# Linear attention and a long convolution on one core: rows regrouped by nine, heads stacked in pairs, the inverse transform by two half sums

## The chip, the cores and the metric

The kernel runs on one core of one Trainium2 chip. The metric is the device time of one execution in microseconds (us); lower is better. A core has five engines that run on their own and wait for each other by semaphores: TensorE (PE in the profile, with its weight loads shown as PEld), VectorE (DVE), ScalarE (ACT), GpSimd (POOL) and SyncE (SP). Matmuls accumulate in PSUM, eight banks of 128 partitions by 512 fp32 numbers. Loads that change fp32 into bf16 are issued from POOL's queue, transposes by DMA and the stores from SP's queue.

## The reference

```python
def phi(x):                                  # q, k, v: batch 8, heads 8, seq 576, head_dim 64
    proj = x @ w_phi                         # 64 -> 128 features
    proj = proj - max(abs(proj), axis=-1)
    return concat([exp(proj), exp(-proj)])
q_p, k_p = phi(q), phi(k)
kv  = k_p.T @ v        # per head, 256 x 64
z   = sum(k_p, over s)
x   = (q_p @ kv) / (q_p @ z + 1e-6)          # heads side by side: batch 8, seq 576, 512
x1, x2, x3 = split(x @ w_proj)               # 512 -> 3 * 512
conv = irfft(rfft(x2) * rfft(filter))        # along the sequence, length 576
out  = (x1 * conv * x3) @ w_out              # 512 -> 512, float32
```

## The kernel before

The program is one list of words, `PLAN`, and `run` (line 874) carries out the words one after another; each word is a method of `Kernel` that issues a few instructions, and `@n` names the PSUM bank. The order of the words is thus the order of the instructions on each engine, and an engine takes its instructions strictly in that order. Work of two batches is interleaved: while batch b goes through the projections and the convolution, batch b+1 goes through the attention.

**Attention of a batch.** `load` and `loadt` (L492, L499) bring k, q and v on POOL's queue, `tr` and `trt` (L505, L512) transpose k and q on SP's queue. 576 rows do not divide into tiles of 128 rows, so row s = 4p+j of the first 512 rows sits on partition p, and the last 64 rows of the eight heads are "tail" tensors of their own (`knt`, `kTt`, `Etp`, `vtp`, `xnt`, ...). `Pk` and `Qn` (L522) project k and q through w_phi; `maxk` and `maxq` (L582, L595) take the absolute maxima on DVE; `ex` (L570) the exponentials on ACT. The maximum of q has to be taken away inside the exponential: `mhi` and `mlo` split it into two bf16 parts, `trm` (L622) transposes them by DMA into `mT`, and `Pq` (L549, L553) adds them by a small matmul. `mT` is therefore the gate into the second half of a batch's attention, and its eight transposes mark the eight batches in the profile. `em` and `vs` (L627, L635) scale v; `KV` (L663, L666) forms k_p.T @ [v, 1] with all 128 rows as contraction plus a tail matmul, `NE` (L684) multiplies with q_p, `rc` and `xn` (L698, L703) divide, `trx` (L722) transposes the result by DMA into `xT`.

**Projections and convolution.** The Fourier transform is cut by parity: `fold` (L739, POOL) forms sums and differences of the two halves of the sequence, `X2` (L755, PE) projects them, `F` (L434) multiplies with the cosine and sine matrices `fwd`, with `Fe` copying to `C`. `m1`, `m2` and `m3` (L771, L779, L785) multiply with the filter's spectrum, `A` and `B`: m1 on DVE, m2 on POOL, their sum m3 on DVE into `Y`. `I` (L837) is the inverse transform over all 512 first rows, with five matmuls of 512 columns for each quarter of the features, and `It` (L844) the same for the 64 tail rows. `X1`, `X3` (L791), `X1t`, `X3t` (L798) are the two gates: `X1e` copies the first, `tm` (L827) multiplies it with the second into `ts`, `ym` (L848) multiplies `I`'s result with `ts`, `O` (L858) multiplies with w_out in five pieces a batch, the fifth with 64 rows only, and `Oe` and `st` write out.

**Setup.** The transform matrices are made on the chip (`gen_*`), the filter is loaded by 26 DMAs on SP's queue ahead of the first transposes (L402, L407), folded on POOL and transformed (`H`).

Number of buffers (`RING`): two each of `kn`, `qn`, `vn`, `xn`, `xT`; one each of `kT`, `qT`, `eo`, `x2n`, `C`, `t1`, `t2`, `Y`, `x1s`, `ts`, `yT`.

Of the kernel before, what the change touches and what calls it, by code (L numbers as in the profile page):

```python
# [19 lines left out]
RING = {'Ekp': 4, 'Ekm': 4, 'Eqp': 3, 'Eqm': 3, 'vp': 3, 'vm': 3, 'r': 4, 'o': 4, 'kn': 2, 'qn': 2, 'vn': 2, 'knt': 2, 'qnt': 2, 'vnt': 2, 'mk': 2, 'mkt': 2, 'mq': 2, 'mh': 2, 'mT': 2, 'xT': 2, 'xTt': 2, 'KVs': 2, 'vtp': 2, 'vtm': 2, 'Etp': 2, 'Etm': 2, 'etp': 2, 'etm': 2, 'rt': 2, 'kTt': 2, 'qTt': 2, 'xnt': 2, 'xn': 2}  # L20
# [16 lines left out]
Pq,0,3@4 rc,0,0@2 xn,0,0@2 loadt,q,2 ex,q,m,0,3@4 tr,q,1 NE,0,2@6 trx,0,0 rc,0,2@6 Pk,1,1@0 xn,0,2@6
NEt,0@2 ex,q,p,0,3@4 trt,q,1 trx,0,2 Pk,1,0@6 maxk,1,1@0 loadt,k,2 NE,0,3@4 ex,k,m,1,0@6 rc,0,3@4
xn,0,3@4 ex,k,p,1,0@6 load,k,3 trx,0,3 Pk,1,2@4 rct,0@2 xnt,0,1@2 ex,k,p,1,2@4 load,q,3 xnt,0,0@2
trxt,0 Qn,1,0@2 maxk,1,0@6 loadt,q,3 ex,k,p,1,1@0 maxq,1,0@2 Qn,1,1@6 em,p,1,0 fold,0,1 em,m,1,0  # L40
ex,k,m,1,1@0 maxq,1,1@6 trt,k,1 X1,0,0@2 ex,k,m,1,2@4 Qnt,1@0 maxqt,1@0 Qn,1,2@6 foldt,0,1 X2,0,2@3
maxk,1,2@4 X1e,ACT,0,0@2 foldt,0,0 X2,0,3@0 vs,p,1,0 X2e,ACT,0,2@3 maxq,1,2@6 X2e,ACT,0,3@0 X2,0,4@1
X2e,ACT,0,4@1 Qn,1,3@4 maxq,1,3@4 Pk,1,3@2 X1,0,1@0 fold,0,0 ex,k,m,1,3@2 tr,k,2 F,0,2@6 mhi,1
maxk,1,3@2 Fe,ACT,0,2@6 F,0,3@7 X2,0,1@1 X1e,ACT,0,1@0 vs,m,1,0 Fe,DVE,0,3@7 X2,0,0@4 em,m,1,1
X2e,ACT,0,1@1 X2e,ACT,0,0@4 X3,0,1@5 mlo,1 vs,m,1,1 trm,1 F,0,1@6 tm,0,1@5 em,p,1,1 ex,k,p,1,3@2
Pkt,1@0 F,0,4@7 trt,q,2 maxkt,1@0 Fe,ACT,0,1@6 emt,p,1 vs,p,1,1 trt,k,2 F,0,0@4 emt,m,1 Fe,DVE,0,4@7
Fe,ACT,0,0@4 Pqt,1@0 Pq,1,1@2 ext,m,1@0 Pq,1,0@6 vst,p,1 X3,0,0@5 ext,p,1@0 X1,0,2@4 tm,0,0@5
vst,m,1 ex,q,m,1,1@2 X1e,DVE,0,2@4 Pq,1,2@0 X3,0,2@5 m1,0,1 ex,q,m,1,2@0 load,v,3 KV,1,1@4 m1,0,2
# [12 lines left out]
X2,1,0@2 maxk,2,2@4 vs,m,2,0 X2e,ACT,1,0@2 F,1,2@3 maxq,2,2@6 Fe,ACT,1,2@3 Pk,2,3@0 F,1,1@4 tr,k,3
# [855 lines left out]
```

## Time and profile before

| | |
|---|---|
| time, median of 3 runs | 421.32 us (417.97 to 423.01) |
| the profiled execution's own time | 419.22 us |
| its span in the profile | 417.2 us |
| granted TensorE clock, mean | 0.942 |
| matmuls | 3367 |
| DMA: packets, moved | 111598, 43.90 MB |
| of these smaller than 512 B | 80648 |

A line of a group names the line in the code, the engine, the operation, what it writes and reads, shapes and count; then the busy time of all of them in us and the mean duration of one in ns, then the engine's idle time just ahead of them and what ended it. A line of a stretch gives its length, then for PE, PEld, DVE, ACT and POOL the busy us and the number of instructions, the granted TensorE clock, the mean busy share of the 16 DMA engines (over 1 where transfers queue) and GB/s. A timeline line gives start and duration in us; for SP's queue the duration is that of the issue, not of the transfer. A line of the chain gives start, duration, and line of a piece of the chain that ended last.

### The profile page before, as it was taken

How to read it: one execution, taken by the hardware profiler on the slowest of the kernel's cores; microseconds unless marked ns; L12 is line 12 of the kernel's file. 1: busy time of each engine (PE TensorE's matmuls, PEld its weight loads, DVE VectorE, ACT ScalarE, POOL GpSimd, SP SyncE). 2: the span in 40 equal slices, each digit the busy share in tenths (PEclk: the TensorE clock that was granted, in tenths of full speed). 3: DMA queues.
4: the chain of work that ended last, by engine and by line, in shares of the span. 5: the costliest groups of instructions: out<-in, count | busy, mean ns of one | idle time of the engine just before them, and what ended most of it. 6: DMA issues, size and time to landing. Idle time of an engine off the chain costs nothing. (4 is left out here: it accounts for less than half of the span.)

```text
span 417.2 us, 8401 instructions
## 1 busy us (share of the span) xinstructions
PE 323.1 (77%) x3367; PEld 176.0 (42%) x3367; DVE 270.1 (65%) x426; ACT 222.5 (53%) x340; POOL 226.7 (54%) x237
## 2 busy tenths in 40 slices
PE   5001277079696988779979979588999999989995
PEld 5001137034462446434635545234654564446452
DVE  3605945355884776925857999537889788876172
ACT  1201677528535637646816777246656756765532
POOL 8580738089924893078725780378428805760540
PEclk9999997559898999969989999979999999999999
DMA  9999959984989377856896394814833234103403
GB/s 157 221 194 183 123 92 117 133 113 85 118 104 162 72 97 71 130 129 80 98 157 152 74 115 77 155 41 81 111 83 102 53 70 128 42 2 46 126 2 113
DMA packets 111598, 43.90 MB, mean 105 GB/s; under 512 B 80648, under 2 KB 105736, under 8 KB 111560
## 3 DMA queue, kind: packets, MB, share of 16 engines
q0 software_dynamic: 39232, 16.29, 33.9%
q1 hardware_dynamic: 72328, 27.08, 32.9%
q8 instruction: 26, 0.43, 0.4%
q14 instruction: 12, 0.10, 0.1%
HBM read 34.01 MB, written 9.44 MB: 104 GB/s over the span
## 5 line engine op out<-in xcount | busy, mean ns | idle before, releaser
L791 PE MATMUL ps<-xT,wproj 128*128 128x512 bf16 x256 | 66.5, 393 | 10.7 <-DMA xT<-xn 8.2
L595 DVE TENSOR_REDUCE mq<-ps 128x8 f32<-128x1024 f32 x32 | 38.5, 1219 | 31.8 <-PE ps L522 27.0
L582 DVE TENSOR_REDUCE mk<-ps 128x8 f32<-128x1024 f32 x32 | 38.6, 1216 | 26.0 <-PE ps L522 20.6
L739 POOL TENSOR_TENSOR eo<-xT 128x896 bf16<-128x896 bf16 x16 | 30.1, 1885 | 36.3 <-DMA xT<-xn 36.3
L755 PE MATMUL ps<-wproj,eo 128*128 128x512 bf16 (+1 forms) x160 | 41.9, 405 | 6.0 <-POOL eo L739 5.9
L779 POOL TENSOR_TENSOR t<-C,B 128x512 bf16<-128x512 bf16 x32 | 38.8, 1228 | 13.5 <-ACT C L671 11.3
L570 ACT ACTIVATE Ekm<-ps 128x1024 bf16<-128x1024 f32 x32 | 32.4, 1023 | 20.8 <-PE ps L522 20.2
L570 ACT ACTIVATE Ekp<-ps 128x1024 bf16<-128x1024 f32 x32 | 32.4, 1020 | 20.5 <-PE ps L522 15.6
L570 ACT ACTIVATE Eqm<-ps 128x1024 bf16<-128x1024 f32 x32 | 32.5, 1031 | 17.1 <-PE ps L553 17.1
L837 PE MATMUL ps<-inv,Y 128*128 128x512 bf16 x160 | 39.5, 388 | 1.6 <-DVE Y L785 1.6
L635 POOL TENSOR_TENSOR vp<-vn,vp 128x1024 bf16<-128x1024 bf16 x16 | 30.8, 1930 | 15.9 <-ACT vp L627 15.8
L858 PE MATMUL ps<-wout,yT 128*128 128x512 bf16 x160 | 38.9, 386 | 0.0
L791 PEld LDWEIGHTS <-wproj 128*128 128x128 bf16 x256 | 23.1, 99 | 29.3 <-issue 6.8
L492 POOL DMA_DIRECT2D qn<-in_q_dram x8 | 7.3, 912 | 51.1 <-DMA qT<-qn 41.9
L671 ACT COPY o<-ps 128x512 f32<-128x512 f32 (+1 forms) x31 | 18.1, 585 | 31.1 <-PE ps L858 24.3
L522 PE MATMUL ps<-wphi,qT 64*128 64x128 bf16 x256 | 14.5, 245 | 25.7 <-DMA qT<-qn 21.0
L434 PE MATMUL ps<-x2n,fwd 128*128 128x512 bf16 (+1 forms) x136 | 34.1, 380 | 0.0
L522 PE MATMUL ps<-wphi,kT 64*128 64x128 bf16 x256 | 13.3, 235 | 26.2 <-DMA kT<-kn 24.1
L635 POOL TENSOR_TENSOR vm<-vn,vm 128x1024 bf16<-128x1024 bf16 x16 | 31.3, 1954 | 4.1 <-ACT vm L627 4.1
L570 ACT ACTIVATE Eqp<-ps 128x1024 bf16<-128x1024 f32 x32 | 32.5, 1033 | 1.0 <-PE ps L553 1.0
L671 ACT CAST x1s<-ps 128x512 bf16<-128x512 f32 (+1 forms) x24 | 13.2, 550 | 31.6 <-PE ps L791 30.0
L748 POOL TENSOR_TENSOR eo<-xT,xTt 128x128 bf16<-128x128 bf16 x32 | 12.8, 424 | 30.1 <-DMA xTt<-xnt 18.3
(149 smaller groups left out, 739.0 us busy)
## 6 DMA issues: line engine op xcount, KB each, us to landing
out_dram<-o SPq DMA_DIRECT2D x32, 256.0 KB, 2.7
kn<-in_k_dram POOLq DMA_DIRECT2D x8, 512.0 KB, 7.1
qn<-in_q_dram POOLq DMA_DIRECT2D x8, 512.0 KB, 7.2
vn<-in_v_dram POOLq DMA_DIRECT2D x8, 512.0 KB, 6.6
wproj<-in_moe_w_proj_dram POOLq DMA_DIRECT2D x1, 1536.0 KB, 13.1
out_dram<-o SPq DMA_DIRECT2D x8, 128.0 KB, 2.3
fl<-in_moe_filter_fft_dram SPq DMA_DIRECT2D x6, 112.0 KB
fl<-in_moe_filter_fft_dram SPq DMA_DIRECT2D x18, 32.0 KB, 5.1
```

Source lines behind the costliest of these rows:

```text
L434: self.mm(self.pb(0), l, r, start=(i == 0), stop=(i == len(ks) - 1))
L570: self.nc.scalar.activation(self.at("E" + n + g, i).rearrange("p a b c f -> p a (b c f)"), self.db(), AF.Exp, bias=0.0, scale=1.0 if g == ...
L582: self.nc.vector.tensor_reduce(out=o, in_=self.db().rearrange("p a (w j f) -> p a w j f", w=2, j=2), axis=AX.X, op=ALU.max, apply_absolute ...
L595: self.nc.vector.tensor_reduce(out=o, in_=self.db().rearrange("p a (w j f) -> p a w j f", w=2, j=2), axis=AX.X, op=ALU.max, apply_absolute ...
L635: self.nc.gpsimd.tensor_tensor(out=t[:, :, :, 0:64], in0=vn[:, 4 * X:4 * X + 4], in1=t[:, :, :, 64:65].to_broadcast([128, 4, 4, 64]), op=A ...
L671: self.nc.scalar.copy(dst, src)
L739: self.nc.gpsimd.tensor_tensor(out=o, in0=x[:, :, :, 0:56], in1=x[:, :, :, 72:128], op=op)
L755: self.mm(self.pb(0, p1=n), eo[:, kt, a:a + n], w[:, kt, 512:1024], start=(kt == 0), stop=(kt == 3))
L779: self.nc.gpsimd.tensor_tensor(out=self.at("t2", b)[:, t, :], in0=self.at("C", b)[:, t ^ 1, :], in1=self.at("B")[:, t, :], op=ALU.mult)
L791: self.mm(self.pb(0), w[:, kt, f0 + 128 * m:f0 + 128 * m + 128], x[:, kt, :], start=(kt == 0), stop=(kt == 3))
L837: self.mm(self.pb(0), Y[:, t, 128 * m:128 * m + 128], inv[:, t, 0:512], start=(t == 0), stop=(t == 4))
L858: self.mm(self.pb(0), y[:, kt, 128 * j:128 * j + 128], w[:, kt, :], start=(kt == 0), stop=(kt == 3))
```

## The change

- **Rows.** Row s = 9t+j, t from 0 to 63, j from 0 to 8. A tile of 128 partitions holds 64 values of t for two adjacent heads, one head above the other. All 576 rows are then in the main tensors, and the tail tensors `knt`, `qnt`, `vnt`, `kTt`, `qTt`, `vtp`, `vtm` and the words `loadt`, `trt`, `emt`, `vst` go; j = 8 is kept apart only where a tile of eight is full (`Fkp`, `Fqp`, `xnt`). A load of k, q or v reads 2304 consecutive bytes a piece, 512 pieces, where it read 1024 pieces of 1024 bytes and, for the tail, 512 pieces of 256 bytes.
- **KV** contracts each head over its 64 partitions: 72 matmuls of 64 rows for two pairs of heads, the two halves of the array in turn, 1152 in all, where there were 640 of 128 rows.
- **Pq** adds the maxima by eight matmuls of 128 columns where there were four of 256.
- **Fold and F.** Halves of the sequence now differ in t, by 32; `X2` has four pieces of 128 rows and one of 64, so that the last matmul of each `F` contracts 64 rows.
- **Inverse transform by half sums.** `I` computes the even and the odd frequencies for half of the sequence, 288 columns each, into two banks: six matmuls of 288 columns where there were five of 512 and five of 64. `Ie` (ACT) copies the even part to SBUF in fp32; `Ip` and `Im` (DVE) write sum and difference, the two halves of the sequence, into `cv`; `ym` multiplies `cv` with the gate product, 25 of 32 on POOL. `It` and `ymt` go.
- **Spectrum.** `m1` reads `F`'s result from PSUM and writes `Y`; `m3` adds `t2` in place, 14 of 16 on POOL. `t1` goes; `ts` goes too, since `tm` now writes in place into `x1s`.
- **Output tails of two batches** share one `O` of 128 rows: 36 pieces in place of 40, with a copy `yt` into the odd batch's partner.
- **Buffers.** `kT` gets two, `xn` one, `yT` two.
- **Order.** The list is a new one. The first k and q come in halves, q's maxima come ahead of k's, `w_phi` comes on SP's queue, w_proj in four pieces later on, and `hold`, a one-element copy on POOL, lets the loads of the next batch start only when the first q has been transposed.

```diff
-RING = {'Ekp': 4, ..., 'kn': 2, 'qn': 2, 'vn': 2, ..., 'xT': 2, 'xTt': 2, ..., 'xn': 2}
+RING = {'Ekp': 4, ..., 'kn': 2, 'qn': 2, 'vn': 2, 'kT': 2, ..., 'xn': 1, 'yT': 2, ..., 'es': 2, 'cv': 2}
-load,k,0 gen_phase filt_load gen_rows zeros gen_half load,q,0 gen_cols@0 w_load,phi load,v,0
+gen_phase loadh,k,0,1 loadh,q,0,1 loadh,q,0,0 gen_rows gen_half gen_cols@0 gen_cols_ev@0 gen_angles
+gen_sin loadh,k,0,0 filt_load,SP,0 w_load,phi w_phi trh,q,0,1 Qn,0,3@0 trh,q,0,0 hold,q,0 trh,k,0,0
...
+    def hold(self, n, b):
+        self.nc.gpsimd.tensor_copy(self.at("junk"), self.at(n + "T", b)[0:1, 17, 0:1])
...
     def load(self, n, b):
-        src = self.dram[n][b]
-        main = src[:, 0:512, :].rearrange("h (p j) d -> p h (j d)", j=4)
         self.nc.gpsimd.dma_start(
-            out=self.at(n + "n", b).rearrange("p (h x) -> p h x", h=8), in_=main)
+            out=self.at(n + "n", b).rearrange("p v j d -> p v (j d)"),
+            in_=self.dram[n][b].rearrange("h (t j) d -> (h t) (j d)", j=9).rearrange(
+                "(v p) x -> p v x", p=128))
...
+    def KV(self, b, X):
+        for w in range(2):
+            v = 2 * X + w
+            for s, g in enumerate("pm"):
+                E, Ft = self.at("Ek" + g, 4 * b + v), self.at("Fk" + g, b)
+                vg = self.at("v" + g, 2 * b + X)
+                a = (2 * w + s) * 65
+                for j in range(9):
+                    for u in range(2):
+                        r = slice(64 * u, 64 * u + 64)
+                        e = E[r, j % 2, j // 2, :] if j < 8 else Ft[r, w, X, :]
+                        self.mm(self.pb(u, a, a + 65), e, vg[r, w, j, :], start=(j == 0),
+                                stop=(j == 8))
...
-    def m1(self, b, i):
...
+    def m1(self, b, t):
+        self.nc.vector.tensor_tensor(out=self.at("Y", b)[:, t, :], in0=self.pb(0), in1=self.at("A")[:, t, :],
+                                     op=ALU.mult)
...
+    def m3(self, eng, b, i):
         s = slice(2 * i, 2 * i + 2)
+        e = self.nc.vector if eng == "DVE" else self.nc.gpsimd
+        Y = self.at("Y", b)[:, s, :]
+        e.tensor_tensor(out=Y, in0=Y, in1=self.at("t2", b)[:, s, :], op=ALU.add)
...
     def I(self, b, m):
         Y, inv = self.at("Y", b), self.at("inv")
-        for t in range(5):
-            self.mm(self.pb(0), Y[:, t, 128 * m:128 * m + 128], inv[:, t, 0:512],
-                    start=(t == 0), stop=(t == 4))
...
+        for e in range(2):
+            for i, t in enumerate((2 * e, 2 * e + 1, 4)):
+                self.mm(self.pb(e, 0, 288), Y[:, t, 128 * m:128 * m + 128], inv[:, e, i, :],
+                        start=(i == 0), stop=(i == 2))
+
+    def Ie(self, b, m):
+        self.nc.scalar.copy(self.at("es", 4 * b + m), self.pb(0, 0, 288))
+
+    def half_sum(self, b, m, odd):
+        e = self.at("es", 4 * b + m).rearrange("p (j t) -> p j t", j=9)
+        o = self.pb(1, 0, 288).rearrange("p (j t) -> p j t", j=9)
+        self.nc.vector.tensor_tensor(out=self.at("cv", 4 * b + m)[:, :, odd, :], in0=e, in1=o,
+                                     op=ALU.subtract if odd else ALU.add)
...
-    def ym(self, b, m):
-        self.nc.vector.tensor_tensor(out=self.at("yT", b)[:, m, 0:512], in0=self.pb(0),
-                                     in1=self.at("ts", b)[:, m, 0:512], op=ALU.mult)
...
+    def ym(self, eng, b, m):
+        e = self.nc.vector if eng == "DVE" else self.nc.gpsimd
+        e.tensor_tensor(out=self.at("yT", b)[:, m, 0:SEQ],
+                        in0=self.at("cv", 4 * b + m).rearrange("p j h t -> p (j h t)"),
+                        in1=self.at("x1s", b)[:, m, :], op=ALU.mult)
...
     def O(self, b, j):
-        y, w = self.at("yT", b), self.at("wout")
+        y, w = self.at("yT", b - (j == 4)), self.at("wout")
```

Two places show how the order moves. The first is the head of SP's queue: `fl` are the filter's pieces, `kT`, `qT` the transposes of k and q, `fwd` and `fwdh` the transform matrices, `mT` the first maxima. Before:

```order
L402 DMA fl_175<-in_moe_filter_fft_dram 40x512
L402 DMA fl_175<-in_moe_filter_fft_dram 56x512
L407 DMA fl_175<-in_moe_filter_fft_dram 16x512 x8
L505 DMA_TRANSPOSE kT_90<-kn_79 128x16x128
L505 DMA_TRANSPOSE qT_87<-qn_75 128x16x128
L512 DMA_TRANSPOSE kTt_91<-knt_81 128x2x128
L365 DMA_TRANSPOSE fwd_66<-G 128x3x128 x4
L366 DMA_TRANSPOSE fwd_67<-G_171 128x5x128
L367 DMA_TRANSPOSE fwdh_68<-G_171 128x5x128
L512 DMA_TRANSPOSE qTt_88<-qnt_77 128x2x128
L622 DMA_TRANSPOSE mT_101<-mh_99 128x5x128
```

The same queue now, from its first transfer:

```order
L383 DMA fl_203<-in_moe_filter_fft_dram 32x512 x8
L385 DMA fl_203<-in_moe_filter_fft_dram 32x512 x2
L443 DMA phi<-in_w_phi_dram 64x128 x2
L490 DMA_TRANSPOSE qT_81<-qn_75 128x9x128 x2
L490 DMA_TRANSPOSE kT_82<-kn_77 128x9x128 x2
L383 DMA fl_204<-in_moe_filter_fft_dram 32x512 x8
L385 DMA fl_204<-in_moe_filter_fft_dram 32x512 x2
L363 DMA_TRANSPOSE fwd_66<-G 128x3x128 x2
L605 DMA_TRANSPOSE mT_90<-mh_88 128x128
```

Twelve transfers stand ahead of the first transpose where 26 stood, and the first `mT` stands ahead of the second batch's k and of four of the six matrices.

The second place is POOL's queue in the middle of the program, where one batch goes through the convolution. Before, `eo` is the fold, `vp`, `vm` the scaled v, `t` the product m2, `vtp`, `vtm` the tail's v:

```order
L739 TENSOR_TENSOR eo_549<-xT_147 128x4x224
L635 TENSOR_TENSOR vp_112<-vn_84,vp_112 128x16x64
L635 TENSOR_TENSOR vm_128<-vn_84,vm_128 128x16x64
L779 TENSOR_TENSOR t_553<-C_551,B_71 128x512 x2
L648 TENSOR_TENSOR vtp_116<-etp_118,vmask_74 128x8
L650 TENSOR_TENSOR vtp_116<-vnt_86,vtp_116 128x8x64
L635 TENSOR_TENSOR vp_113<-vn_84,vp_113 128x16x64
L648 TENSOR_TENSOR vtm_132<-etm_134,vmask_74 128x8
L650 TENSOR_TENSOR vtm_132<-vnt_86,vtm_132 128x8x64
L635 TENSOR_TENSOR vm_129<-vn_84,vm_129 128x16x64
L492 DMA vn_84<-in_v_dram 128x8x256
L779 TENSOR_TENSOR t_553<-C_551,B_71 128x512
```

The same engine now, where `Y` is the sum m3 and `yT` the product `ym`:

```order
L737 TENSOR_TENSOR t_794<-C_793,B_71 128x512 x2
L745 TENSOR_TENSOR Y_795<-Y_795,t_794 128x1024
L737 TENSOR_TENSOR t_794<-C_793,B_71 128x512
L745 TENSOR_TENSOR Y_795<-Y_795,t_794 128x1024
L474 DMA vn_79<-in_v_dram 128x4x576
L474 DMA kn_77<-in_k_dram 128x4x576
L818 TENSOR_TENSOR yT_801<-cv_800,x1s_796 128x576
L818 TENSOR_TENSOR yT_801<-cv_799,x1s_796 128x576
```

The tail's products have gone from POOL, and m3 and `ym`, which DVE had, stand between m2, the loads and the next fold, which follows after one more `ym`; `I` waits for the `Y` and `O` for the `yT` that POOL writes here.

More of the change, by code (lines that the diff above doesn't have):

```diff
@@ L169 @@
+Oe,ACT,6,1@1 st,6,1 Ip,7,3@4 ym,DVE,7,3 yt,DVE,7 O,7,0@1 Oe,ACT,7,0@1 st,7,0 O,7,1@0 O,7,2@1
+Oe,DVE,7,2@1 Oe,ACT,7,1@0 st,7,1 st,7,2 O,7,3@0 Oe,ACT,7,3@0 st,7,3 O,7,4@4 Oe,ACT,7,4@4 st,7,4
 """
@@ new lines, in Pqt @@
+    def Pqt(self, b):
+        x, w, sel, mT = self.at("qT", b), self.at("wphi"), self.at("sel"), self.at("mT", b)
+        for y in range(2):
+            r, k = self.half(y, 8)
+            self.mm(self.pb(y, 0, 256), w[r, :], x[r, k:k + 10:9, :], start=True, stop=False)
+        for X in range(2):
+            for y in range(2):
+                r = slice(64 * y, 64 * y + 64)
+                self.mm(self.pb(y, 128 * X, 128 * X + 128), sel[r, 16 + X, :], mT[r, :],
+                        start=False, stop=(X == 1))
```

844 lines of the change are left out of this document (384 added, 460 removed).

## The prediction

> **What bounds the kernel now.** First the page, for the engines' totals:
>
> ```profile
> span 417.2 us, 8401 instructions
> PE 323.1 (77%) x3367; PEld 176.0 (42%) x3367; DVE 270.1 (65%) x426; ACT 222.5 (53%) x340; POOL 226.7 (54%) x237
> ```
>
> No engine is full over the whole span, so I cut it where the eight `mT` transposes stand in SP's timeline (57.9, 97.2, ... 360.1 us) and ask for the engines' busy time in each stretch:
>
> ```profile
> 0.00:57.90 57.90, 16.53 (x119) 11.76 (x120) 29.30 (x71) 16.74 (x27) 30.68 (x40) 1.00 1.10 164
> 57.90:97.20 39.30, 22.65 (x282) 14.46 (x282) 18.07 (x28) 22.49 (x35) 23.65 (x29) 0.70 1.07 123
> 97.20:149.20 52.00, 44.30 (x462) 23.10 (x461) 34.61 (x50) 28.79 (x45) 36.62 (x37) 0.93 0.75 101
> 149.20:190.70 41.50, 34.25 (x365) 17.90 (x363) 27.19 (x42) 23.87 (x35) 20.45 (x23) 0.92 0.72 110
> 190.70:234.80 44.10, 40.44 (x427) 21.26 (x425) 31.37 (x48) 25.96 (x43) 26.60 (x28) 0.96 0.73 115
> 234.80:283.40 48.60, 39.31 (x433) 21.06 (x433) 34.80 (x47) 26.89 (x41) 26.16 (x26) 0.93 0.61 103
> 283.40:321.50 38.10, 35.66 (x395) 19.40 (x392) 32.32 (x48) 23.51 (x36) 20.43 (x20) 1.00 0.47 90
> 321.50:360.10 38.60, 38.36 (x417) 20.38 (x415) 31.93 (x50) 25.23 (x39) 21.11 (x19) 1.00 0.34 79
> 360.10:417.20 57.10, 51.55 (x481) 26.69 (x479) 30.53 (x49) 29.02 (x47) 20.98 (x19) 0.99 0.22 56
> ```
>
> Three regimes. Up to 97 us the DMA engines are oversubscribed (shares 1.10 and 1.07) and PE works 39 of 97 us. From 283 us PE is the bound: 38.36 of 38.60 us at clock 1.00, one batch in about 38.4 us. Between them PE lacks some time and some clock. After 97.2 us PE is busy 283.9 of 320.0 us (seven rows added): 36 us idle, and with clocks of 0.92 to 0.96 about 11 us lost to the clock (each row's busy time by what its clock lacks). So of 417 us some 58 are spent on PE's waits before 97 us and 47 on waits and clock after.
>
> What ends the waits, from the waits of PE after 97 us, the waits of all engines over the whole span, and SP's timeline:
>
> ```profile
> PE ps L791 <- DMA xT<-xn: 8.2, 2, 4.8
> PE ps L755 <- POOL eo L739: 5.6, 1, 5.6
> PE ps L522 <- DMA qT<-qn: 3.6, 3, 2.5
> PE ps L565 <- DMA mT<-mh: 2.8, 2, 1.7
> ...
> POOL qn L492 <- DMA qT<-qn: 41.9, 4, 13.0
> POOL eo L739 <- DMA xT<-xn: 36.3, 3, 15.3
> PE ps L522 <- DMA kT<-kn: 24.1, 1, 24.1
> ...
> 2.82 5.62 SPq L407 DMA_DIRECT2D fl<-in_moe_filter_fft_dram  x8
> 17.99 9.32 SPq L505 DMA_TRANSPOSE kT<-kn  x1
> 27.41 8.15 SPq L505 DMA_TRANSPOSE qT<-qn  x1
> 57.87 1.20 SPq L622 DMA_TRANSPOSE mT<-mh  x1
> 257.02 1.92 SPq L505 DMA_TRANSPOSE qT<-qn  x1
> ```
>
> The first transpose can go only at 18 us, behind 26 filter pieces, and then takes 9.3 us to issue where an uncrowded one takes 1.9. 20 us of PE's later waits end with a DMA, the fold's 5.6 among them, since the fold itself waits for `xT`.
>
> **The change, part by part.** *The start.* Before, PE gets k at 35 us and `mT` goes at 57.9. Now q comes first, in halves, with twelve transfers ahead of it on SP and `hold` keeping the second batch's loads back. Two chains lead to the first `mT`.
>
> ```profile
> 15.59 2.26 DVE L339 TENSOR_TENSOR turn<-turn,whole 128x2016 f32<-128x2016 f32 x1
> ...
> L595 DVE TENSOR_REDUCE mq<-ps 128x8 f32<-128x1024 f32 x32 | 38.5, 1219 | 31.8 <-PE ps L522 27.0
> ```
>
> On DVE, the copy of w_phi, without which PE can't begin, stands behind the angles, which end at 17.9; then four maxima of 1.22 us and a short one of about half that (5.5), then `gen_five` and `gen_sel`, some 17 small instructions, an estimate of 5 us at 0.3 each, under the 0.42 that 260 columns cost in the row of KVs below: 28.5. On SP: twelve pieces at 0.7 (5.62/8) are 8.4; four half transposes at 1.0 to 4.7 each (half of 1.92 and of 9.32); ten more pieces, 7; two matrices, 3, at less than the 1.92 of a whole q: 23 uncrowded, 38 crowded. I take 31, near the free price, because `hold` removes the crowding. From the first `mT` to the second, the data sets the pace: k, q of two batches and one v are 5.9 MB, the filter 1.2; at the 164 GB/s of the first stretch 43 us, then a transpose, the projection and five maxima, so 57 at the earliest. DVE has some 30 us of work there (nine maxima 11, the spectrum's five copies, inv, KV and xn of batch 0). I take 36 us against 39.3 before, so the second `mT` stands at 67 in place of 97.2: **-30**. Bounds: 61 (28.5 + 32) to 83 (31 + 52, the longest stretch above).
>
> *PE's work.* The chain that ended last gives rates at full clock, and a timeline of PE at 355 us the rate of two half arrays in turn (lines 522 and 553 contract 64 rows; 375.61 follows a line 553):
>
> ```profile
> 375.61 1.19 PE ps L837 x5
> 376.80 0.13 PE ps L663 x4
> 380.93 1.08 PE ps L837 x5
> 382.01 0.58 PE ps L844 x20
> 383.09 4.32 PE ps L858 x20
> ...
> 355.73 0.40 PE L522 MATMUL ps<-wphi,qT 64*128 64x128 bf16 x8
> 356.06 1.06 PE L755 MATMUL ps<-wproj,eo 128*96 128x512 bf16 x4
> ```
>
> A matmul of 512 columns costs 0.216 us, one of 65 0.0325, one of 64 0.029. Inverse transform: before 160 x 0.216 + 160 x 0.029 = 39.2; now 192 of 288 columns, 0.1215 each in proportion, 23.3: -15.9. Output: 16 fewer, -3.5. Pq has the same columns: 0. KV goes from 640 x 0.0325 = 20.8 to 1152 matmuls on half arrays, a form that no row shows. Eight of L522 take 0.33 us to the next instruction, less one switch (below) 0.22, so 0.0275 each with 128 columns; with 65 it is between half of 0.0325, if two halves run fully side by side, and 0.0325. I take the L522 rate, since it is the nearest form: 31.7, **+10.9** (bounds -2.1 to +16.6). The Trainium skill (TensorE: Matmul & The Clock Gate, section "Wait — 56ns, not 53.3ns?") puts a floor of about 25 ns between starts of matmuls however short; by it KV would cost 28.8, and the term +8.0. No row here goes below 0.0275, which agrees.
>
> The five matmuls of L837 take 1.19 us behind a 64-row form and 1.08 elsewhere: a change between 64 and 128 rows costs 0.11. Going through the list, such changes rise from 168 to 226: the 64-row piece at the end of each F adds two, less those next to another 64-row form. +6.4, at least 0. The Trainium skill (TensorEngine Tiling, section "Tiling Modes") says that a change of tiling mode drains the array. It speaks against this F, and the row's 0.11 agrees. Sum for PE: -2, bounds -21.5 and +3.6.
>
> *DVE, ACT, POOL.*
>
> ```profile
> L848 DVE TENSOR_TENSOR yT<-ps,ts 128x512 bf16<-128x512 f32 x32 | 21.8, 688 | 8.0 <-PE ps L837 6.8 <-ACT Eqp L570 0.8
> L785 DVE TENSOR_TENSOR Y<-t,t 128x1024 bf16<-128x1024 bf16 x16 | 13.9, 880 | 0.3
> L771 DVE TENSOR_TENSOR t<-C,A 128x1024 bf16<-128x1024 bf16 x16 | 21.1, 1324 | 5.8 <-ACT C L671 5.8
> L673 DVE CAST KVs<-ps 128x260 bf16<-128x260 f32 x20 | 8.4, 424 | 12.0 <-PE ps L666 11.6
> L671 ACT CAST KVs<-ps 128x260 bf16<-128x260 f32 x12 | 4.5, 376 | 5.4 <-PE ps L666 5.3
> L635 POOL TENSOR_TENSOR vm<-vn,vm 128x1024 bf16<-128x1024 bf16 x16 | 31.3, 1954 | 4.1 <-ACT vm L627 4.1
> L779 POOL TENSOR_TENSOR t<-C,B 128x512 bf16<-128x512 bf16 x32 | 38.8, 1228 | 13.5 <-ACT C L671 11.3
> L739 POOL TENSOR_TENSOR eo<-xT 128x896 bf16<-128x896 bf16 x16 | 30.1, 1885 | 36.3 <-DMA xT<-xn 36.3
> ```
>
> DVE gains 64 half sums (0.424 at 260 columns, so about 0.45 at 288: +28.9) and m1 from PSUM (40 of L848's form, 27.5, for 21.1 and a fifth piece a batch before), loses nearly all of m3 and of ym (-36 with the tails): about the same. ACT gains 32 copies of about 0.4 (+12.8) and has 17 fewer copies of 512 columns, at no more than twice 0.376, and seven fewer of 260 (-2.6): the same. POOL gains ym (25 x 1.228 x 576/512 = 34.5), m3 (14 x 1.95 = 27.3), an eighth on vs (+7.8) and on the fold (+4.4), and loses the tail's products (21) and half of its issues (some 35): 227 to 245. All three stay under PE's need, so I cost them at nothing; what hides them is PE's 38 us a batch, of which POOL fills 30. Where they stand on the path, at the end, I, Ie, half sums and ym replace I and ym: +2.
>
> *Waits after the second mT.* Pieces loaded for k, q, v fall from 36,864 to 12,288 with the same bytes; kT's second buffer lets k be transposed before PE has finished. Between nothing (bytes decide) and all 47, I take half of the 20 us of DMA-ended waits and half of the clock's 11: **-15**.
>
> Sum on the profiled execution's 419.2 (span 417.2): -30 -2 +2 -15 = **374**. The median of 421.3 lies 0.5% above that execution, inside the spread of the runs.
>
> **The rivals.** *Start only (390).* The xT waits end with a chain of xn, a transpose and a fold, not with a full DMA queue, and POOL's longer queue stands before the fold. Then the 15 us don't come: 389; with the start at its worse bound 83, 405. For it: the DMA shares are 0.75 and less after 97 us, and PE waits all the same.
>
> *PE gets lighter (354).* Half arrays fully side by side and no cost for F's switch: -21.5 instead of -2, so 374 - 20. Against it the 0.0275 and the 0.11.
>
> *POOL takes PE's place (slower, 437).* POOL stands idle 190 us now, 78 of them in the two waits quoted (L492 behind qT, L739 behind xT). Behind the first stand mostly further loads; now m3 and ym stand among the loads, which I and O need. If POOL keeps its idle time beside 245 busy, the span is 435, the time 437. It decides from the point where POOL keeps over 172 us of its idle time. Against it: k's second buffer, and waits that PE's faster pace shortens.
>
> **How the numbers follow.** Forecast 374: 0.58. Start only: 0.20. Lighter PE: 0.15. POOL: 0.07. A measurement of this kernel can tell about 1%, 4 us. Only the last is slower; of "start only" I put 0.02 within 1%, if the start reaches its worse bound and POOL's queue adds a little. So faster 0.91, same 0.02, slower 0.07. The range, 350 to 402, takes in lighter PE and most of start only, up to near its 405; outside stay POOL's case and small parts of the others.
>
> **What would show it.** The first mT near 31 us and the second near 67; KV at about 0.0275 us a matmul; the matmuls of 288 columns near 0.12; in the middle, PE idle well under 36 us with a clock above 0.95; POOL near 245 busy. I am wrong if the first mT comes after 40 us, if PE waits mostly for POOL's Y or yT, or if the stretches between mT stay at 42 us or more.

## The result, and the profile after

| | before | after |
|---|---|---|
| time, median, the two kernels run in turn on one chip | 422.16 us | 376.69 us |
| ratio after to before | | 0.8927, 95% interval 0.8848 to 0.9005 |
| the same, repeated later on one chip | 419.04 us | 375.26 us, 0.8952 (0.8899 to 0.9004) |
| the profiled execution's own time | 419.22 us | 378.21 us |
| its span | 417.2 us | 376.4 us |
| granted TensorE clock, mean | 0.942 | 0.951 |

The forecast was 374 us. Of some kernels below a few executions ran some per cent longer; the ratios leave those out, and of the kernel with one `kT` a single execution remains, so it has no ratio.

The page of the changed kernel, its totals and its two large DMA queues (packets, MB, share of 16 engines; q0 carries the loads of k, q and v, q1 the transposes and stores):

```profile
span 376.4 us, 9310 instructions
PE 303.6 (81%) x3816; PEld 171.1 (45%) x3863; DVE 273.8 (73%) x450; ACT 219.1 (58%) x346; POOL 241.2 (64%) x184
q1 hardware_dynamic: 68320, 25.97, 38.3%
q0 software_dynamic: 13808, 16.25, 28.4%
```

The same stretches as in the prediction, cut where the eight `mT` transposes stand in SP's timeline (columns as there: length, then busy us of PE, PEld, DVE, ACT, POOL, granted clock, DMA share, GB/s):

```profile
0.00:36.75 36.75, 10.89 (x94) 9.88 (x94) 23.00 (x51) 10.62 (x14) 16.25 (x25) 1.00 1.03 172
36.75:70.90 34.15, 23.40 (x464) 16.09 (x467) 26.23 (x41) 22.84 (x35) 18.09 (x15) 0.90 0.80 118
70.90:119.40 48.50, 38.14 (x384) 19.24 (x389) 28.69 (x48) 25.85 (x38) 32.48 (x25) 0.86 0.89 141
119.40:160.80 41.40, 38.96 (x481) 20.61 (x484) 34.23 (x54) 28.77 (x50) 33.14 (x22) 1.00 0.80 119
160.80:200.00 39.20, 33.92 (x450) 18.45 (x456) 29.21 (x49) 22.52 (x35) 25.35 (x21) 0.91 0.81 135
200.00:243.30 43.30, 38.12 (x509) 21.45 (x514) 37.27 (x52) 31.62 (x53) 33.62 (x21) 1.00 0.60 113
243.30:281.30 38.00, 35.60 (x460) 19.28 (x466) 30.49 (x48) 25.65 (x41) 25.92 (x19) 0.96 0.45 79
281.30:318.10 36.80, 33.92 (x475) 19.16 (x480) 27.80 (x46) 24.84 (x41) 27.75 (x19) 0.95 0.46 87
318.10:376.40 58.30, 50.69 (x509) 26.91 (x515) 36.87 (x69) 26.41 (x46) 28.57 (x20) 0.98 0.34 75
```

The start shows in SP's timeline: q's first two transposes are issued from 8.09 us and take 4.18 together, where k's was issued at 17.99 and took 9.32 and q's at 27.41 and took 8.15.

```profile
8.09 4.18 SPq L490 DMA_TRANSPOSE qT<-qn  x2
```

The second `mT` goes at 70.9 us where it went at 97.2: 26.3 us. What comes after it is 305.5 us where it was 320.0: 14.5 us. In that part PE's busy time (seven rows added) falls from 283.9 to 269.4 and its idle time stands at 36.1 before and after. One caution: of PE's matmul records 36 are missing in these seven rows (add the counts of PE and of PEld: 3268 against 3304), and a missing matmul reads as idle time. The waits that the profile names are free of that. After the second `mT` they sum to 31.4 us before and 26.7 now, 1.6 of it without a cause that the profile shows. So the waits fell by 0 to 5 us and the work by 10 to 14.5. The trace of a kernel below with the same matmuls (`gen_sel` moved) has all its records, and narrows this. Its stretch after the second `mT`:

```profile
63.88:365.20 301.32, 270.96 (x3302) 144.73 (x3302) 216.88 (x354) 185.98 (x297) 208.48 (x152) 0.95 0.65 108
```

Against 283.9 before, PE's work fell by 12.9 us, so some 1.6 of the 14.5 are left for waits. The largest waits of PE after 70 us in the changed kernel (total, number, longest):

```profile
PE ps L750 <- DMA xT<-xn: 9.8, 3, 4.9
PE ps L516 <- DMA qT<-qn: 3.6, 1, 3.6
PE ps L408 <- DVE x1s L638: 3.0, 1, 3.0
PE ps L523 <- DMA qT<-qn: 2.1, 1, 2.1
PE ps L543 <- DMA mT<-mh: 1.9, 1, 1.9
```

17.4 us end with a DMA; before it was 20.2, with the fold's 5.6. The third row is new: PE waits for a DVE copy that itself was late. POOL ends none of PE's named waits here.

PE's lighter work shows in its timeline at full clock (start, duration, line; L631 is KV) and in the chain that ended last (start, duration, line):

```profile
293.81 0.42 PE L631 MATMUL ps<-vp,Ekp 64*128 64x65 bf16 x16
294.10 0.42 PE L631 MATMUL ps<-vm,Ekm 64*128 64x65 bf16 x16
```

```profile
83.57 0.75 PE ps L408 x3
...
295.34 1.15 PE ps L631 x72
297.37 0.91 PE ps L408 x3
...
336.60 0.73 PE ps L798 x6
```

A group of 18 KV matmuls starts every 0.285 us, and 72 take 1.15: 0.016 us each, where the prediction took 0.0275. A matmul of 288 columns (L798) costs 0.122, as forecast. An F of three matmuls (L408) costs 0.75 in one place and 0.91 in another, where three of 0.216 make 0.65.

### The profile page after: what moved, and what is told of

It reads as the page before. It is cut to its first block, busy times and chain, and to the rows that moved or that the text cites. A ratio compares the mean times of both kernels' runs of the same rounds, so it can differ in the third digit from the quotient of the medians.

```text
span 376.4 us, 9310 instructions
## 1 busy us (share of the span) xinstructions
PE 303.6 (81%) x3816; PEld 171.1 (45%) x3863; DVE 273.8 (73%) x450; ACT 219.1 (58%) x346; POOL 241.2 (64%) x184
## 4 chain that ended last, share of the span: by engine, by line
PE 61%; DMA 18%; DVE 11%; issue 4%; SPq 2%; ACT 2%; POOL 0%; DVEq 0%; ACTq 0%; POOLq 0%
PE ps L750 14%; PE ps L719 9%; PE ps L408 8%; PE ps L830 6%; DMA qT<-qn 6%; PE ps L631 5%; DMA xT<-xn 5%; PE ps L652 4%; PE ps L798 4%; DMA kT<-kn 3%; PE ps L543 2%; DMA qn<-in_q_dram 2%; PE ps L537 2%; PE ps L516 2%; DMA mT<-mh 2%
## 5 line engine op out<-in xcount | busy, mean ns | idle before, releaser
L576 DVE TENSOR_REDUCE mq<-ps 128x8 f32<-128x1024 f32 (+1 forms) x40 | 43.5, 1111 | 22.8 <-PE ps L523 12.1
L818 POOL TENSOR_TENSOR yT<-cv,x1s 128x576 bf16<-128x576 f32 x25 | 32.4, 1315 | 25.6 <-DVE cv L807 19.1
L616 POOL TENSOR_TENSOR vm<-vn,vm 128x1152 bf16<-128x1152 bf16 x16 | 34.4, 2152 | 20.4 <-ACT vm L610 20.4
L737 POOL TENSOR_TENSOR t<-C,B 128x512 bf16<-128x512 bf16 x32 | 36.4, 1154 | 14.5 <-ACT C L636 7.2
L707 POOL TENSOR_TENSOR eo<-xT 128x1024 bf16<-128x1024 bf16 x16 | 35.0, 2196 | 16.1 <-DMA xT<-xn 9.9
L576 DVE TENSOR_REDUCE mk<-ps 128x8 f32<-128x1024 f32 (+1 forms) x40 | 43.7, 1110 | 2.1 <-PE ps L523 0.6
L616 POOL TENSOR_TENSOR vp<-vn,vp 128x1152 bf16<-128x1152 bf16 x16 | 34.4, 2152 | 12.5 <-ACT vp L610 8.8
L408 PE MATMUL ps<-x2n,fwd 128*128 128x512 bf16 (+1 forms) x121 | 38.2, 387 | 4.7 <-DVE x1s L638 3.0
L560 ACT ACTIVATE Ekp<-ps 128x1024 bf16<-128x1024 f32 x32 | 32.8, 1030 | 14.5 <-PE ps L509 13.2
L830 PE MATMUL ps<-wout,yT 128*128 128x512 bf16 x132 | 36.8, 396 | 3.1 <-ACT x1s L636 1.4
L719 PE MATMUL ps<-wproj,eo 128*128 128x512 bf16 x154 | 39.0, 383 | 0.4 <-issue 0.2
L745 POOL TENSOR_TENSOR Y<-Y,t 128x1024 bf16<-128x1024 bf16 x14 | 29.7, 2125 | 2.2 <-DVE Y L733 0.9
L733 DVE TENSOR_TENSOR Y<-ps,A 128x512 bf16<-128x512 f32 x40 | 26.6, 682 | 5.4 <-PE ps L408 5.2
L807 DVE TENSOR_TENSOR cv<-es,ps 128x288 f32<-128x288 f32 x64 | 25.4, 447 | 4.2 <-ACT es L802 2.3
L798 PE MATMUL ps<-inv,Y 128*128 128x288 bf16 x192 | 28.3, 291 | 0.0
```

Of the source, the lines that this page charges most:

```text
L408: self.mm(self.pb(0), l, r, start=(i == 0), stop=(i == len(ks) - 1))
L560: self.nc.scalar.activation(e, self.db(), AF.Exp, bias=0.0, scale=1.0 if g == "p" else -1.0)
L576: self.nc.vector.tensor_reduce(out=out, in_=src, axis=AX.X, op=ALU.max, apply_absolute_value=True)
L616: self.nc.gpsimd.tensor_tensor(out=t[:, :, :, 0:64], in0=self.at("vn", b)[:, 2 * X:2 * X + 2], in1=t[:, :, :, 64:65].to_broadcast([128, 2, ...
L707: self.nc.gpsimd.tensor_tensor(out=o, in0=x[:, :, :, 0, :], in1=x[:, :, :, 1, :], op=op)
L719: self.mm(self.pb(0), eo[:, kt, 128 * c:128 * c + 128], w[:, kt, 512:1024], start=(kt == 0), stop=(kt == 3))
```

## The experiments

All ratios are to the kernel before, run in turn with each kernel on the same chip; the base to compare with is the changed kernel's 0.895.

### KV's halves one after the other

```diff
-                for j in range(9):
-                    for u in range(2):
+                for u in range(2):
+                    for j in range(9):
```

> The changed kernel with one edit: in KV the nine matmuls of one half of the array come first and then the nine of the other, where the halves took turns. Same matmuls, same results. Theory, that the two halves run fully side by side when they take turns (18 matmuls of 65 columns in 0.285 us, 0.016 each): serial they cost 0.0275 to 0.0325 each, 1152 x 0.0115 to 0.0165 = 13 to 19 us more PE work, and the time rises by 8 to 19 us to a ratio of 0.91 to 0.94, since PE is the bound of most stretches. Rival, that 0.016 is only what one short matmul costs in this trace: same rate in either order, ratio 0.89, and PE's lighter load has another source.

Measured: 382.92 us, ratio 0.9164 (0.9097 to 0.9231). KV in the chain of this kernel, near full clock:

```profile
251.29 1.55 PE ps L631 x72
```

0.0215 us a matmul instead of 0.016, about 6 us over 1152, and the time rose by 6 to 10 us. So the rate does come from the two halves running beside each other, and the rival falls. The size was missed: even with nine matmuls of one half in a row, PE did not go back to 0.0275 or more. Starts of the next group's matmuls on the idle half (`vm`) stand in the trace among those of the running one (`vp`), so that the halves still overlap in part:

```profile
296.25 0.19 PE L631 MATMUL ps<-vp,Ekp 64*128 64x65 bf16 x1
296.27 0.19 PE L631 MATMUL ps<-vm,Ekm 64*128 64x65 bf16 x1
```

### F's last matmul on 128 rows

```diff
-                  (f[0:64, 2, :], src[0:64, 4, :])]
+                  (f[0:n, 2, :], src[0:n, 4, :])]        # n = 128 for F, 64 for H
...
-        n = 64 if c == 4 else 128
-        self.copy(eng, self.at("x2n", b)[0:n, c, :], self.pb(0, p1=n))
+        self.copy(eng, self.at("x2n", b)[:, c, :], self.pb(0))
```

> The changed kernel, but the last matmul of each F contracts 128 rows with zeros below the 64 real ones, so that PE stays in one form (X2e copies all 128 rows of piece 4). Theory as in the prediction, 0.11 us for a change between the 64- and the 128-row form: up to 80 changes less, 6 to 9 us less PE work, and 3 to 8 us less time (ratio 0.873 to 0.885). Rival, that a change costs nothing beside work that is queued, or that a full array at 128 rows draws more clock: no change, ratio 0.89.

Measured: 373.18 us, ratio 0.8908 (0.8835 to 0.898), inside the base's interval: too small to tell alone. It comes back below in the kernel that joins three edits, where the F of three matmuls in the same two places of the chain read:

```profile
70.90 0.65 PE ps L410 x3
...
278.49 0.81 PE ps L410 x3
```

0.65 against 0.75, and 0.81 against 0.91: leaving the full array and coming back costs 0.10 us an F, so 0.05 for each of the two changes. What the further 0.16 of the second place comes from is not shown. In the order of their weight loads the traces have 225 changes between the 64- and the 128-row form in the changed kernel and 169 with the wide F, 56 less and not 80, since beside some F another 64-row form stands anyway: 2.8 us. The prediction had 0.11 for each of 58 changes, 6.4.

### q first, and mlo ahead of the setup's other DVE work

```diff
-Pk,0,2@0 ... filt_load,SP,1 Qnt,0@4 maxqt,0@4 maxq,0,0@6 Pk,0,1@4 ... gen_selidx gen_five gen_sel Pkt
+zeros Qnt,0@4 maxq,0,0@6 maxqt,0@4 mhi,0 mlo,0 Pk,0,2@0 ... filt_load,SP,1 trm,0 Pk,0,1@4 ... gen_selidx gen_sel gen_five Pkt
```

> The changed kernel with q's last projection and maxima ahead of k's second piece, and mlo ahead of gen_five, gen_sel and POOL's fold of the filter: nothing on the way to the first mT waits for k any longer. The first mT should go at 28 to 31 us in place of 36.75. Theory A, the first mT sets the start: everything after it comes 5 to 8 us earlier, time 369 to 372, ratio 0.875 to 0.882. Theory B, the second batch's q sets it (its transpose goes at 48.6 us, behind loads that the data rate sets): the second mT stays at 69 to 71 us and the time falls by less than 2 us.

Measured: 374.17 us, ratio 0.8952 (0.8889 to 0.9016), the base's. The first `mT` went at 25.1 us, nearly 12 us earlier than in the changed kernel's profile, and the second at 71.3. Theory A falls: the first `mT` carries nothing to the end. Theory B's outcome holds, but its reason (q's loads) was not what the next runs showed.

### mlo on POOL

```diff
-        self.nc.vector.tensor_tensor(out=m[:, :, 1, 0:18], ...
+        self.nc.gpsimd.tensor_tensor(out=m[:, :, 1, 0:18], ...
```

> The changed kernel with mlo (36 elements, the last step before each mT) on POOL in place of DVE. Theory, that DVE's mlo is held up while POOL runs an instruction on two SBUF operands (it took 1440 ns on average, up to 4950, and ended just as vs ended on POOL): the 10 us that the eight lose go, other DVE instructions keep their lengths, and the time falls by 1 to 6 us (ratio 0.878 to 0.89). Rival, that mlo then only waits in POOL's own order behind vs and the fold, or that POOL's queue now waits for the maxima: no change, or 1 to 3 us slower.

What led to it, in the changed kernel's timeline of DVE and of POOL (start, duration, engine, line):

```profile
238.32 4.95 DVE L601 TENSOR_TENSOR mh<-mq,mh 128x36 bf16<-128x36 f32 x1 [0.44 <-ACT mh L597]
...
238.94 4.26 POOL L616 TENSOR_TENSOR vp<-vn,vp 128x1152 bf16<-128x1152 bf16 x2
```

Both end within 0.1 us of each other at 243.2. The `mlo` began 0.6 us ahead of the first `vp`, while POOL issued a load; what held it for that part is not shown. All eight `mlo` of the changed kernel, and the eight of this one:

```profile
L601 DVE TENSOR_TENSOR mh<-mq,mh 128x36 bf16<-128x36 f32 x8 | 11.5, 1440 | 3.3 <-ACT mh L597 3.3
```

```profile
L601 POOL TENSOR_TENSOR mh<-mq,mh 128x36 bf16<-128x36 f32 x8 | 2.0, 252 | 25.4 <-ACT mh L597 25.4
```

Measured: 368.9 us, ratio 0.8836 (0.8763 to 0.891): 1.2% under the base, some 5 us, at the fast end of the theory, though the two intervals touch. PE's wait for the late DVE copy is gone, and its named waits after the second `mT` sum to 21.8 us. The rival, that POOL's queue would lose as much, falls. The first `mT` went at 25.4 us and the second still at 69.8. Between them, DVE and POOL of this kernel:

```profile
26.63 5.13 DVE L465 TENSOR_SCALAR selone<-selidx 128x18 f32<-128x18 f32 x4
...
26.78 1.28 POOL L390 TENSOR_TENSOR fe<-fl,fl 128x512 bf16<-128x512 f32 x1
28.01 1.27 POOL L391 TENSOR_TENSOR fe<-fl,fl 128x512 bf16<-128x512 f32 x1
```

Four instructions of `gen_sel`, 18 elements each, took 5.13 us, while POOL ran four folds of the filter (two are shown). `Pq` can't start before `sel` is made.

### gen_sel where POOL is idle

```diff
-... gen_rows gen_half gen_cols@0 ...      ... gen_selidx gen_five gen_sel Pkt,0@6 ...
+... gen_rows gen_half gen_selidx gen_sel gen_cols@0 ...      ... gen_five Pkt,0@6 ...
```

with `mlo` on POOL, and with `Qnt`, `maxqt` and the last `maxq` of batch 0 ahead of `Pk,0,2`.

> The changed kernel with mlo on POOL, and in the setup gen_sel (which took 10 us on DVE beside the filter's fold on POOL, 5.1 of it for four instructions of 18 elements that take 0.39 alone) ahead of the matmuls for the columns, where DVE stands idle, and q's last projection ahead of k's second piece. Theory, that between the first and the second mT the path went through gen_sel held up by POOL's fold: the second mT moves from 69.8 to 59 to 64 us, and the time falls by another 5 to 10 us against mlo on POOL alone (ratio 0.86 to 0.872). Rival, that the second batch's q (data rate) sets the second mT: it stays at 68 to 71 us, ratio 0.884.

Measured: 366.47 us, ratio 0.8729 (0.8682 to 0.8776). The same four instructions:

```profile
5.61 0.41 DVE L465 TENSOR_SCALAR selone<-selidx 128x18 f32<-128x18 f32 x4 [1.27 <-POOL selidx L458]
```

0.41 in place of 5.13, and the second `mT` moved from 69.8 to 63.9, so q's loads did not hold it at 69.8. Two things were moved at once; but q's last projection had been moved alone with `mlo` above, and the second `mT` stayed at 71.3 there, so the path went through `gen_sel`. Of these 5.9 us, 1.1% of the time before (4.5 us) arrived by the ratios, 2.4 us by the medians; the ratio lies just above the range of the theory, and its interval overlaps that of `mlo` on POOL alone. Against the base the two edits together are clear: 0.8729 for 0.8952.

### Loads cut in three

```diff
+        for c in range(3):
             self.nc.gpsimd.dma_start(
-                out=....rearrange("p v j d -> p v (j d)"),
+                out=....rearrange("p v j d -> p v (j d)")[:, :, 192 * c:192 * c + 192],
```

> The changed kernel, but each whole load of k, q and v is cut into three by columns, so that its pieces read 768 bytes where they read 2304: three times as many pieces, as many as the kernel before had, at the same bytes, and two more issues on POOL for each load. Theory after the result: PE's waits of 36 us after the second mT did not shrink when the pieces did, because they end a chain (xn, transpose, fold) and not a full queue; then the time rises by at most what the issues on POOL cost, 0 to 4 us (ratio 0.893 to 0.903). The prediction's term (fewer pieces relieve the queues): DMA waits grow again, 5 to 15 us, ratio 0.905 to 0.93.

Measured: 369.72 us, ratio 0.8821 (0.8763 to 0.8879). Its queue of loads:

```profile
q0 software_dynamic: 37040, 16.26, 38.8%
```

About as many pieces as before the change, a tenth more of all DMA engines' time, and still no slower: 1.3% faster than the base, against both expectations. PE's waits for `qT` fell from 5.7 to 0.6 us, those for `xT` rose from 9.8 to 14.5, and all its named waits after the second `mT` sum to 22.7. So here the fewer, larger pieces of the change are not what made it faster. Why small ones helped is not settled: the granted clock was 0.957 to 0.975 in these executions and 0.945 to 0.962 in the base's, which on some 270 us of PE's work would be about 4 of the 5.5 us (an estimate), and whether that is cause or effect is not shown. They did not help again (last experiment).

### No loads from the fourth batch on

```diff
     def load(self, n, b):
+        if b > 2:
+            return
```

> The changed kernel without the loads of k, q and v from the fourth batch on (b over 2: left out, the work goes on with old data); all transposes by DMA and all computation stay. If transfers of loads crowd the transposes, PE's waits for xT, qT and mT after 120 us nearly go and the time falls by 8 to 15 us (ratio 0.855 to 0.875). If those waits are a chain of latencies, they stay and the time falls by no more than 4 us, about what the 20 issues on POOL and a wait for qn are worth (ratio 0.883 to 0.893).

Measured: 353.84 us, ratio 0.8404 (0.834 to 0.8467), 5.5% below the base and more than the theory of crowding gave. The view is the timeline of SP's and of POOL's queue in the changed kernel, where L486 is `tr` and L474 `load`:

```profile
174.73 0.81 POOL L474 DMA_DIRECT2D vn<-in_v_dram  x1
175.53 0.75 POOL L474 DMA_DIRECT2D kn<-in_k_dram  x1
...
175.85 7.84 SPq L486 DMA_TRANSPOSE qT<-qn  x1
```

and the same transpose in the kernel without loads:

```profile
169.27 2.49 SPq L488 DMA_TRANSPOSE qT<-qn  x1
```

Two loads go out 1.1 and 0.3 us ahead of q's transpose, whose issue then holds SP for 7.8 us in place of 2.5, with two `xT` transposes and the stores behind it; PE waits 3.6 us for `qT` there. Without loads PE's named waits after the second `mT` fall from 25.9 us (the base's second profile) to 10.3. The only one of them that ends with a DMA is `xT`, and all of it stands before 116 us, in the batch beside which the last loads still go out (at 96.43 us):

```profile
PE ps L752 <- DMA xT<-xn: 6.3, 2, 3.8
```

After that PE waits for no DMA at all here, against 9.0 us after 119 us in the changed kernel and 10.6 after 113 in the base's second profile. So the waits of that part come from the loads, and my reading after the result, that they are a chain of latencies, is wrong. SP's transposes of q and k themselves wait for a load only once after the second `mT` in the changed kernel, 2.3 us, which speaks for the traffic beside them rather than for the arrival of their data. Not all of the 21 us is shown to be this: 15.6 are named waits of PE, and the granted clock was 0.972 to 0.979 where the base had 0.945 to 0.962, on 270 us of PE's work another 6 or so (an estimate).

### m3 and ym back on DVE

```diff
-m3,POOL ... ym,POOL      (14 and 25 words of the list)
+m3,DVE ... ym,DVE
```

> One part of the change undone: all m3 and ym on DVE instead of POOL. POOL loses some 62 us of work, DVE gains about 14 x 0.9 + 25 x 0.98 = 37, to 310 of 376. If POOL's queue were what holds the kernel (the prediction's slower rival), this would be faster by several us. Theory, POOL does not bind, DVE is the next one behind PE in every batch, and DVE's instructions on two SBUF operands are held up while POOL works: slower by 4 to 15 us (ratio 0.90 to 0.93).

Measured: 405.31 us, ratio 0.9621 (0.9551 to 0.969). The two largest waits of PE in the profiled execution, which took 408.93 us:

```profile
PE ps L798 <- DVE Y L745: 15.1, 7, 3.6
PE ps L516 <- DVE mq L576: 12.9, 3, 7.5
```

Right in sign, and about twice the largest size expected: some 28 us of the change's 44 are lost when DVE has to do what POOL took over. The forms of `ym` differ too: 1343 ns each on average in this kernel, where the few on DVE in the changed kernel took 980.

### One buffer for kT

```diff
-'kT': 2
+'kT': 1
```

> One part of the change undone: one buffer for kT in place of two, so that a k can be transposed only when PE has finished with the last one. The prediction counted the second buffer among what makes waits shorter. If it does, PE's waits grow by a transpose's latency in several batches: 5 to 20 us slower than the changed kernel (ratio 0.905 to 0.94). If transposes of k are issued late anyway, in SP's order and behind the loads, within 3 us.

In this order of the list some `Pk` then read the next batch's k, so that part of the result is computed from other data; the work is the same. Measured: 372.71 us in the one execution that can be compared, against 372.08 to 376.26 us of the base in the same call. In its trace PE's named waits after the second `mT` sum to 25.2 us, where the base's second profile has 25.9, so no cost is seen there. But its other three executions took 381.6 to 389.4 us, within the range of the first expectation. One execution decides nothing: inconclusive, and what the second buffer is worth stays open.

### The base again, and what beats it

> The changed kernel itself, unedited, timed beside the next three on the same chip, as their base. Theory: ratio 0.885 to 0.895 as before; PE idle some 36 us after the second mT, DVE's mlo some 9 to 13 us in all.

Measured: 375.26 us, ratio 0.8952 (0.8899 to 0.9004), `mlo` 11.6 us in all, as expected. Named waits 25.9 us.

> mlo on POOL, gen_sel early, and F's last matmul on 128 rows: the earlier three edits together. If the 0.11 us for a change of form is real time on PE, this is 3 to 6 us below mlo and sel alone (0.8729): ratio 0.857 to 0.866. If the waits or the clock take it back, 0.868 to 0.873.

This kernel joins three edits above: `mlo` on POOL, `gen_sel` early, F's last matmul on 128 rows. Measured: 359.71 us, ratio 0.8615 (0.8564 to 0.8665), so 0.962 of the changed kernel and the fastest of all kernels here that leave nothing out. Its page:

```profile
span 356.3 us, 9306 instructions
PE 297.7 (84%) x3816; PEld 173.4 (49%) x3863; DVE 261.2 (73%) x442; ACT 219.2 (62%) x346; POOL 241.6 (68%) x192
```

Against `mlo` and `gen_sel` alone (0.8729) the wider F brings 1.1% of the time before, 4.8 us; the 2.8 of 56 x 0.05 lie within the intervals.

> The same and each whole load in three, as in the run of split loads, which came out at 0.8821 instead of the 0.893 or more that both theories gave. If small pieces let the transposes through (their issues for q on SP fell from 27.9 to 16.1 us there), this is 2 to 6 us faster than the combination without them. If that run was only lucky in its clock (0.965 against 0.951), no faster, or 1 to 4 us slower for the 44 further issues on POOL.

The same with loads cut in three. Measured: 370.59 us, ratio 0.8837 (0.8782 to 0.8892): 9 to 11 us slower, outside both expectations. The page's totals and PE's waits:

```profile
PE 299.6 (81%) x3816; PEld 174.7 (47%) x3863; DVE 265.3 (72%) x442; ACT 219.2 (59%) x346; POOL 274.3 (74%) x236
```

```profile
PE ps L722 <- POOL eo L710: 7.8, 3, 3.6
...
PE ps L800 <- POOL Y L747: 1.7, 1, 1.7
PE ps L634 <- POOL vp L619: 1.1, 2, 0.8
```

With 32 us more on POOL, all of it issues, PE waits 10.6 us for what POOL makes, where it waits 2.8 without the cut. That is how the prediction's slower rival would look, but POOL's total does not decide it. In the kernel with the loads cut alone POOL was just as busy, and there PE waited for none of its results after the second `mT`:

```profile
PE 303.0 (83%) x3863; PEld 169.7 (46%) x3863; DVE 274.1 (75%) x450; ACT 219.0 (60%) x346; POOL 272.5 (74%) x228
```

Besides, 5.1 of the 12.1 us between the two spans stand before the second `mT`, which went at 69.4 in place of 64.3. Why the same cut costs time here and none there stays open.

## Why the prediction was right, and which steps were not

The forecast of 374 us came within 1% of 376.7. That closeness is in good part luck: of its four terms two were badly sized, PE's work and the waits, and their errors cancelled.

- **Start, -30: measured -26.3.** The second `mT` stood at 70.9, within 61 to 83. No run undoes the new head of SP's queue or `hold`, so that these bring the time is read from the two traces and not shown by an experiment. The reason given for the 36 us between first and second `mT`, that the data rate sets the pace, failed: with `gen_sel` moved away from POOL's fold, with `mlo` on POOL and q's last projection first, the second `mT` went at 63.9 with the same loads. The working had `gen_five` and `gen_sel` at 0.3 us an instruction, and beside POOL's folds four of them took 5.13. The first `mT` came at 36.75 instead of 31; it didn't matter, since at 25 us the second came no earlier.
- **PE's work, -2: measured about -17 over the whole span (323.1 to 306.0 us, in the trace with all records), -12.9 of it after the second `mT`.** The inverse transform came as computed (0.122 for 0.1215). KV was mis-sized: +10.9 in the sum, while 1152 x 0.016 = 18.4 against 20.8 makes -2.4, the lower bound. The step that failed is "I take the L522 rate, since it is the nearest form". That row has 128 columns; at 0.216 for 512, 128 columns alone cost 0.054, so its 0.0275 already is two halves fully side by side. Scaled to 65 columns it gives 0.014, close to the half of 0.0325 that the working named as the lower bound. The Trainium skill says as much (TensorE: Matmul & The Clock Gate, section "The mechanism"): matmuls on different row groups overlap; the runs agree. Its floor of about 25 ns between starts, which the prediction cited from the same page, did not hold for two halves in turn. F's changes of form were some 2.8 us and not 6.4.
- **Waits and clock after the second mT, -15: measured 0 to -5, by the complete trace about -2.** Busy time by what the clock lacked is 12.5 us after and was 11 before. The mechanism named, pieces that relieve the queues, failed: with three times the pieces PE's named waits did not grow, 22.7 us for 26.7. What the working also named, kT's second buffer, stays open. That the loads crowd the transposes is true: some 16 us of PE's named waits went with them. But the change moves the same bytes, so the lower bound, "bytes decide", was the answer.
- **End, +2: measured +1.2** (57.1 to 58.3 us after the last `mT`, PE's work there included).
- **DVE, ACT, POOL at nothing.** POOL's 245 came as 241.2, and POOL did not hold PE. DVE's total was right, 270 to 274, but not that it was free: small DVE instructions beside POOL's work cost about 5 us by the ratios.

Added up by stretch, -26.3 (start) -12.9 (PE after it) -1.6 (all that is left, the end included) make -40.8 on 419.2, that is 378.4, for 378.2 in the profiled execution; the forecast had -30 -2 +2 -15. So both faster and slower rivals on either side of the forecast, "lighter PE" by its half arrays and "start only" by its waits, were true at once. The slower rival, POOL, was not: no named wait of PE ends with POOL in the changed kernel. Of the signs named, the second `mT`, the 288-column matmuls and POOL's total came; KV's rate and the idle time "well under 36 us" did not, and the six stretches between later `mT` came at 36.8 to 48.5 us, 41.2 on average, for 43.8 before.

## What to carry to other kernels

Scale a row's time by its columns before taking it for another form, and ask what it would cost on the whole array: a rate that is half of that already shows two halves at work. A term that rests on transfers needs the quantity that matters, bytes or pieces; a kernel that leaves the loads out, and one that cuts them smaller, tell them apart in two runs. Read the mean duration of the smallest instructions of a group: one of 36 elements at 1.4 us is waiting for something that no list of waits names.

## What the runs showed of the hardware that was not expected

- **DVE held up by POOL inside an instruction.** `mlo`, 36 elements, took 0.19 to 4.95 us; four instructions of 18 elements took 0.41 us alone and 5.13 beside POOL's folds of 1.28. On POOL `mlo` took 0.25. The Trainium skill (SBUF — State Buffer, section "SBUF: two separate sides") says that a DVE instruction in a two-port mode, or one with two SBUF inputs against a GpSimd instruction that reads SBUF, and the GpSimd instruction shut each other out: the one that starts first keeps the shared ports for its whole length. These rows agree, but for the 0.6 us by which the longest `mlo` began before POOL's first `vp`. The profile counts the time as DVE busy, and the kernel with the two edits that avoid it has 0.8729 where the base has 0.8952.
- **Two halves of the array** gave 0.016 us for a matmul of 65 columns in turn and 0.0215 with nine in a row, both under the 0.0325 of one on the whole array.
- **The issue of a transpose** on SP's queue: the same one took 2.5 us without loads and 7.8 with two loads just issued from POOL, and everything behind it in the queue waited.
